# Attention and two gated feed-forward layers on one core: chunk 2 of layer 0 in block products, x summed by VectorE, a later rounding, and GpSimd in part of the decode

## The chip, the cores and the metric

One of the eight cores of a Trainium2 chip runs the whole program. TensorE (PE) multiplies, VectorE (DVE), ScalarE (ACT) and GpSimd (POOL) work on tiles, SyncE (SP) issues loads; each engine takes its instructions in order, and semaphores tie them together. The metric is the device time of one execution in microseconds, the median of the runs.

## The reference

Sliding-window attention with a few global keys and a distance bias, then two feed-forward layers on its output. The weights come as float64. In short:

```python
a = softmax(q @ k.T / sqrt(D) + bias, masked to local and global keys)   # B=2, H=8, S=768, D=64
x = (a @ v) as 1536 tokens x 512
h = x @ w_in1;  x = (h * sigmoid(h)) @ w_out1           # w_in 512 x 2048, w_out 2048 x 512
h = x @ w_in2;  out = (h * clip(h + 3, 0, 6) / 6) @ w_out2
```

## The kernel before, in words

**Precision.** Each operand of a feed-forward matmul is a pair, a rounded high half and the low half that is left (xh and xl, wih and wil, woh and wol, gh and gl). A product takes three matmuls: high by high, high by low, low by high. A matmul here is 128 x 128 by 512 columns.

**Stages.** Attention runs first, in 16 units, with the first feed-forward chunk already between its steps. A layer has 8 chunks of 256 hidden columns, and the tokens are three blocks of 512. For a chunk, an H piece (L489, 12 matmuls, in a PSUM tile psH) makes 128 hidden rows of a block, the gate follows on ScalarE and VectorE, and a Y piece (L662, 6 matmuls, psY) brings it back to 128 output rows or tokens. Y is copied to a tile st by ScalarE (L687) and added to the tile y by an accumulating DMA from GpSimd's queue (L691).

**Block products.** In chunks for which `fast` says so, blocks 0 and 1 are not made by four H pieces but by seven products of six matmuls (L570, tiles psP, a scheme of the Strassen kind), in the order 1, 6, 5, 7, 2, 4, 3. They use sums of blocks of x (T2, T3, T4 and an overwritten part of xh and xl, made in `block_sums`: L621 on VectorE, roundings L594 or L596 on ScalarE, low halves L599 on VectorE) and sums of weights (`sums`: L169 to L181 and L193). Product 1 goes into chain a; ScalarE copies it to chain b (L575) before product 6 adds to it, and copies b to a tile u after products 6 and 7 (L579, L581). Products 2 and 4 end in gates of block 0; products 5, 7 and 3 and u give block 1. The Y pieces of blocks 1 and 2 of the chunk before (eight after a fast chunk, four otherwise) stand between the products where the list `cuts` puts them. Block 2 is made by two H pieces behind them.

**Decode.** The float64 weights of a chunk come in four pieces (two of w_in, two of w_out), loaded by SP (L87, L90). For each, ScalarE takes the magnitude of the upper word (L103), VectorE clamps, shifts, sets the sign and takes the power (L992, L998, L1004, L1009), scales the lower word (L129), adds (L134), ScalarE rounds to the high half (L145) and the low half is subtracted (L148). The engine of L134 and L148 is GpSimd for the two chunks beside the attention and VectorE otherwise. `load_weights` issues a later piece's load once L129 has read its buffer.

**Order.** The program is a list `stream` of pieces; a slot n of the loop records one piece for TensorE and what has been put down for n: the queue (`at`, `split`), `late`, `rests`, and the decode steps (`slots`), which count back from the first piece of their chunk. In the late part the order on all four engines is that of the recording. `ready` picks the PSUM banks of H and Y pieces. At the end of layer 0, `split` with the table `wait` rounds the new x from y: ScalarE's L596 for xh, VectorE's L599 for xl, two for each block.

Of the kernel before, what the change touches and what calls it, by code (L numbers as in the profile page):

```python
# [10 lines left out]
F32 = mybir.dt.float32  # L11
# [17 lines left out]
def attention_ffn_kernel(ctx, tc, q, k, v, n_global, n_local, w_in1, w_out1, w_in2, w_out2, out):  # L29
# [63 lines left out]
    def decode(n):  # L93
# [2 lines left out]
        t = {}  # L96

        beside_attention = i < 2
        engine = nc.gpsimd if beside_attention else nc.vector

        def upper():
            t["a"] = wpool.tile([P, DW], F32, name=f"da{n}", tag="da", bufs=2)
# [51 lines left out]

    def fast(l, c):

        return c > (2, 1)[l]

    terms = {}

# [446 lines left out]
    def whole_block(b):  # L607

        T["x", b] = late_pool.tile([P, KT, FB], F32, name=f"xf{b}", tag=("g1", "ws")[b])
        h, o = (x.bitcast(F32)[:, :, b * FB:(b + 1) * FB] for x in (xh, xl))  # L610
        nc.sync.dma_start(T["x", b], h)
        nc.gpsimd.dma_start(T["x", b], o, accum_op=ALU.add)

    def block_sums(l, n, n1):

# [32 lines left out]
    def y_piece(l, c, tk, m):  # L648
# [16 lines left out]
        for i, ts, size in parts(n0, n1):  # L665
# [28 lines left out]
                    at(n + 9 + j, lambda j=j: nc.scalar.mul(y[:, j, :], y[:, j, :], 1.0 / 6.0))  # L694
            if c == NCH - 1:

                wait = ((6, 6), (5, 5), (4, 3))[i][m // 2]
                split(n + wait, *(x[:, m - 1:m + 1, n0:n1] for x in (xh, xl)), y, 0.5)


# [4 lines left out]
    for l, c in chunks:  # L705
        first_piece[l, c] = len(stream)
        if fast(l, c):
            p = [(product, l, c, i) for i in (1, 6, 5, 7, 2, 4, 3)]
            y, before = before, []
            cuts = [0, 2, 3, 4, 5, 6, 7, 8] if len(y) == 8 else [0, 1, 2, 3, 3, 4, 4, 4]  # L710
            for i in range(7):
                stream += [p[i]] + y[cuts[i]:cuts[i + 1]]
            h, y = H(l, c, 2), Y(l, c, 0)
            stream += [h[0]] + y[:2] + [h[1]] + y[2:]
            before = Y(l, c, 1) + Y(l, c, 2)
            continue
# [64 lines left out]
    with tc.manual_schedule(engines={E.PE, E.Activation, E.Pool, E.DVE}):  # L781

        first_half.close()
        late_pool = second_half.enter_context(tc.tile_pool(name="late", bufs=1, side="right", reuse_waits="tile"))
        for b in range(2):
            whole_block(b)
        for n in range(end, when(len(stream) - 1) + 2):
            if n == when(first_piece[0, 3]):
                ready[0] = 2
            for l, c, early in ((0, 2, 0), (1, 1, 6)):  # L790
                if n == when(first_piece[l, c]) - early:
                    block_sums(l, n, n + early + 12)
            loop(n)
            if n == PRE + 60:
                general = nc.values_load(flag[0:1, 0:1], min_val=0, max_val=2)
# [246 lines left out]
```

## Time and profile before

| | |
|---|---|
| median of 3 runs | 624.74 us (624.72 to 626.45) |
| profiled execution | 625.65 us, its span 623.5 us |
| TensorE clock granted | 0.998 of full speed |
| attention, with chunk 0 beside it | up to about 130 us |
| chunk 2 of layer 0, first H piece | 165.5 us |
| chunk 3 of layer 0, first product | 198.1 us |
| layer 1, first H piece | 358.1 us |
| chunk 2 of layer 1, first product | 423.0 us |
| last matmul of the last Y piece | 617.8 us |

The times in the trace are microseconds from the span's start. A number in brackets behind a row is idle time of that engine just before the instruction, and the engine, tile and line that ended it. Matmuls overlap, so a row's duration (0.39) is longer than the distance to the next. Line numbers are those of the listing above.

### The profile page before, as it was taken

What the parts mean: (1) busy time and instruction counts of PE and PEld (TensorE: products, weight loads), DVE (VectorE), ACT (ScalarE), POOL (GpSimd) and SP (SyncE); (2) the same over time, 40 slices, a digit from 0 to 9 for tenths busy, and PEclk for the clock granted to TensorE, in tenths of its full rate; (3) what the DMA queues carried; (4) which work ended last, traced back from release to release, by engine and by line L of the source; (5) the groups of instructions that cost most, each with busy time, mean ns of one, the idle gap of its engine ahead of it and who ended that gap; (6) DMA issues with size and microseconds to landing.
All of it is one profiled execution on the core that took longest, in us unless ns stands there. A gap on an engine that the chain in (4) does not pass through costs nothing.

```text
span 623.5 us, 9408 instructions
## 1 busy us (share of the span) xinstructions
PE 605.3 (97%) x3128; PEld 494.9 (79%) x3128; DVE 470.6 (75%) x1044; ACT 414.7 (67%) x863; POOL 158.0 (25%) x233
## 2 busy tenths in 40 slices
PE   8899999999999999999999989999999999999996
PEld 3577788898887888888888868887788888888885
DVE  6888888725697776767665789987979696969453
ACT  4888888655576666666656766756667676767660
POOL 3877566820111111111111210011111111111100
PEclk9999999999999999999999999999999999999999
DMA  7767655484776768777876772378577868786544
GB/s 176 178 157 167 155 143 124 138 181 114 159 150 153 182 149 183 155 180 155 183 156 147 173 171 70 126 198 189 124 177 157 184 153 181 155 185 138 102 110 165
DMA packets 81622, 97.29 MB, mean 156 GB/s; under 512 B 55456, under 2 KB 55456, under 8 KB 81312
## 3 DMA queue, kind: packets, MB, share of 16 engines
q0 software_dynamic: 12576, 45.09, 38.6%
q1 hardware_dynamic: 68992, 51.53, 28.3%
q8 instruction: 27, 0.44, 0.3%
q14 instruction: 27, 0.22, 0.1%
HBM read 46.27 MB, written 3.15 MB: 79 GB/s over the span
## 4 chain that ended last, share of the span: by engine, by line
PE 36%; issue 25%; POOL 5%; DVE 2%; DMA 2%; ACT 1%; POOLq 0%; ACTq 0%; SPq 0%; DVEq 0%
PE psY L662 20%; PE psH L489 9%; POOL y L691 5%; PE psP_b L570 3%; PE psP_c L570 2%; PE psP_a L570 2%; DMA y<-st 1%; DMA raw<-in_moe_w_in_dram 1%; ACT st L687 0%; DVE g L520 0%; DVE da L1004 0%; DVE wol L148 0%; DVE u L587 0%; DVE dc L134 0%; ACT da L103 0%
## 5 line engine op out<-in xcount | busy, mean ns | idle before, releaser
L691 POOL DMA_DIRECT2D y<-st x78 | 66.9, 857 | 364.6 <-ACT st L687 359.4
L687 ACT COPY st<-psY 128x512 f32<-128x512 f32 x156 | 91.3, 585 | 52.1 <-PE psY L662 48.0
L489 PE MATMUL psH<-xh,wih 128*128 128x512 f32 (+1 forms) x216 | 83.0, 384 | 2.2 <-DVE g L520 1.8
L489 PE MATMUL psH<-xl,wih 128*128 128x512 f32 (+1 forms) x216 | 82.6, 383 | 0.1
L489 PE MATMUL psH<-xh,wil 128*128 128x512 f32 (+1 forms) x216 | 82.5, 382 | 0.0
L662 PE MATMUL psY<-gh,woh 128*128 128x512 f32 (+1 forms) x160 | 61.4, 384 | 0.6 <-DVE mn L379 0.6
L662 PE MATMUL psY<-gh,wol 128*128 128x512 f32 (+1 forms) x160 | 60.6, 379 | 0.0
L662 PE MATMUL psY<-gl,woh 128*128 128x512 f32 (+1 forms) x160 | 60.5, 378 | 0.0
L662 PE MATMUL psY<-woh,gh 128*128 128x512 f32 x144 | 56.1, 390 | 0.4 <-ACT gh L526 0.4
L662 PE MATMUL psY<-woh,gl 128*128 128x512 f32 x144 | 56.1, 390 | 0.2 <-DVE gl L533 0.2
L662 PE MATMUL psY<-wol,gh 128*128 128x512 f32 x144 | 56.0, 389 | 0.0
L383 ACT ACTIVATE z<-z,mn 128x256 f32<-128x256 f32 (+1 forms) x96 | 46.4, 488 | 10.9 <-DVE mn L379 10.6
L393 POOL TENSOR_SCALAR z<-z,sm 128x256 f32<-128x256 f32 (+1 forms) x96 | 43.5, 471 | 32.3 <-DVE sm L389 25.0
L489 PEld LDWEIGHTS psH<-xh,wih 128*128 128x128 f32 x216 | 40.6, 188 | 10.4 <-DVE g L520 2.2
L103 ACT ACTIVATE da<-raw 128x512 f32<-128x512 f32 x64 | 43.0, 672 | 6.8 <-DMA raw<-in_moe_w_in_dram 5.6
L489 PEld LDWEIGHTS psH<-xl,wih 128*128 128x128 f32 x216 | 40.5, 188 | 7.9 <-DVE xl L425 0.5
L1004 DVE SCALAR_TENSOR_TENSOR da<-raw,da 128x512 int32<-128x512 int32 x64 | 46.0, 718 | 1.0
L489 PEld LDWEIGHTS psH<-xh,wil 128*128 128x128 f32 x216 | 40.6, 188 | 7.5 <-POOL wil L148 0.3
L992 DVE TENSOR_SCALAR da<-da 128x512 f32<-128x512 f32 x64 | 29.1, 454 | 16.2 <-ACT da L103 16.1
L587 DVE TENSOR_TENSOR u<-psP_c,u 128x512 f32<-128x512 f32 x22 | 15.1, 687 | 34.5 <-ACT u L581 34.5
L511 ACT ACTIVATE a<-psH 128x512 f32<-128x512 f32 (+1 forms) x24 | 14.2, 590 | 40.5 <-PE psH L489 38.7
L530 DVE SCALAR_TENSOR_TENSOR gl<-a,gh 128x512 fp32r<-128x512 f32 (+1 forms) x34 | 23.2, 681 | 22.3 <-ACT gh L524 22.0
(187 smaller groups left out, 1499.8 us busy)
## 6 DMA issues: line engine op xcount, KB each, us to landing
y<-st POOLq DMA_DIRECT2D x78, 512.0 KB, 4.9
raw<-in_moe_w_in_dram SPq DMA_DIRECT2D x32, 512.0 KB, 4.3
raw<-in_moe_w_out_dram SPq DMA_DIRECT2D x32, 512.0 KB, 3.6
rk<-in_k_dram SPq DMA_DIRECT2D x32, 96.0 KB, 3.2
rq<-in_q_dram SPq DMA_DIRECT2D x32, 96.0 KB, 2.7
rv<-in_v_dram SPq DMA_DIRECT2D x32, 96.0 KB, 2.6
out_dram<-y SPq DMA_DIRECT2D x12, 256.0 KB, 2.3
xf<-xh SPq DMA_DIRECT2D x2, 1024.0 KB, 4.8
```

Of the source, the lines that this page charges most:

```text
L103: nc.scalar.activation(out=t["a"], in_=raws[n][:, :, 1].bitcast(F32), func=AF.Abs)
L383: nc.scalar.activation(out=z[:, t, h, :w], in_=z[:, t, h, :w], func=AF.Exp, bias=mn[:, t, h:h + 1], scale=-1.0, accum_out=sm[:, t, h:h + 1])
L393: nc.gpsimd.tensor_scalar(out=z[:, t, h, :w], in0=z[:, t, h, :w], scalar1=smt[u][:, t, h:h + 1], scalar2=1.0, op0=ALU.mult, op1=ALU.mult)
L489: nc.tensor.matmul(ps, a[:, kt, js], x[:, kt, n0:n1], start=n == 0, stop=n == 3 * KT - 1)
L530: nc.vector.scalar_tensor_tensor(out=gl[:, j, :], in0=t["a"], scalar=2.0, in1=gh[:, j, :].bitcast(F32), op0=ALU.mult, op1=ALU.subtract)
L570: nc.tensor.matmul(ps, a[:, 2 * k + q, f * P:(f + 1) * P], x, start=p in (1, 5) and n == 0, stop=n == 5, skip_group_check=True)
L587: nc.vector.tensor_tensor(out=u, in0=st["c"], in1=u, op=ALU.add)
L662: nc.tensor.matmul(ps[:, :rhs.shape[1]], lhs, rhs, start=n == 0, stop=n == 3 * FC - 1)
L687: nc.scalar.copy(st[:, m % 2, :], part)
L691: late.setdefault(n, []).append(lambda: nc.gpsimd.dma_start(y, st, accum_op=ALU.add))
L992: nc.vector.tensor_scalar(out=a, in0=a, scalar1=as_float(897 << 20), scalar2=as_float((1151 << 20) - 1), op0=ALU.max, op1=ALU.min)
L1004: nc.vector.scalar_tensor_tensor(out=ai, in0=w1, scalar=-0x40000000, in1=ai, op0=ALU.bitwise_and, op1=ALU.bitwise_or)
```

## The change

Four things change.

- `fast` takes in chunk 2 of layer 0. Its blocks 0 and 1 become seven products; the block sums of layer 0 are recorded from the end of the attention on, their last rounding four slots ahead of the chunk, and the banks are switched at chunk 2, not 3. The decode of the chunk gets the lead that fast chunks have, and the weight sums.
- `whole_block` puts xh + xl together with four VectorE instructions of 128 x 1024, where a load on SP's queue and an accumulating DMA on GpSimd's did it for each block.
- `cuts` for four Y pieces puts two of them between product 1 and product 6 and none between product 6 and product 5. The rounding of block 2 of the new x is recorded at slots 5 and 5 behind its Y pieces, not 4 and 3.
- In layer 1, chunks 1 to 3 have L134 and L148 on GpSimd (24 instructions).

```diff
-        engine = nc.gpsimd if beside_attention else nc.vector
+        engine = nc.gpsimd if beside_attention or NCH < i < NCH + 4 else nc.vector
...
-        return c > (2, 1)[l]
+        return c > 1
...
-        nc.sync.dma_start(T["x", b], h)
-        nc.gpsimd.dma_start(T["x", b], o, accum_op=ALU.add)
+        for k in range(0, KT, 2):
+            h, o = (x.bitcast(F32)[:, k:k + 2, b * FB:(b + 1) * FB] for x in (xh, xl))
+            nc.vector.tensor_tensor(out=T["x", b][:, k:k + 2], in0=h, in1=o, op=ALU.add)
...
-                wait = ((6, 6), (5, 5), (4, 3))[i][m // 2]
+                wait = ((6, 6), (5, 5), (5, 5))[i][m // 2]
...
-            cuts = [0, 2, 3, 4, 5, 6, 7, 8] if len(y) == 8 else [0, 1, 2, 3, 3, 4, 4, 4]
+            cuts = [0, 2, 3, 4, 5, 6, 7, 8] if len(y) == 8 else [0, 2, 2, 3, 3, 4, 4, 4]
...
-            if n == when(first_piece[0, 3]):
+            if n == when(first_piece[0, 2]):
                 ready[0] = 2
-            for l, c, early in ((0, 2, 0), (1, 1, 6)):
-                if n == when(first_piece[l, c]) - early:
-                    block_sums(l, n, n + early + 12)
+            if n == end:
+                block_sums(0, n + 1, when(first_piece[0, 2]) - 4)
+            if n == when(first_piece[1, 1]) - 6:
+                block_sums(1, n, n + 18)
```

Three places in the order of instructions show it. The first is ScalarE at the start of chunk 2 of layer 1, from the copy of product 1 (tile psP_2_a) into chain b; st_1_2 are the old Y pieces of block 2. Before:

```order
L575 COPY psP_2_b<-psP_2_a 128x512
L687 COPY st_1_2_0_4789<-psY_1_1024_0_4782 128x512
L579 COPY u_2_4777<-psP_2_b 128x512
L687 COPY st_1_2_0_4789<-psY_1_1024_1_4803 128x512
L103 ACTIVATE da_4818<-raw_4715 128x512
```

and after:

```order
L575 COPY psP_2_b<-psP_2_a 128x512
L687 COPY st_1_2_0_4796<-psY_1_1024_0_4789 128x512
L687 COPY st_1_2_0_4796<-psY_1_1024_1_4800 128x512
L579 COPY u_2_4784<-psP_2_b 128x512
L103 ACTIVATE da_4825<-raw_4722 128x512
```

The copy out of product 6 (L579) has moved behind the second Y piece's copy, as product 6 has on TensorE.

The second is VectorE early in layer 1's chunk 0, where y_2 is the new x of block 2 and g_0_0_1 the gate that frees the second H piece's bank. Before:

```order
L1009 TENSOR_SCALAR de_4254<-da_4186 128x512
L599 SCALAR_TENSOR_TENSOR xl<-y_2_2124,xh 128x2x512
L520 SCALAR_TENSOR_TENSOR g_0_0_1_4259<-a_0_0_1_4251,psH_0_0_1_4238 128x512
L129 SCALAR_TENSOR_TENSOR dc_4279<-raw_4064,de_4254 128x512
L992 TENSOR_SCALAR da_4256<-da_4256 128x512
L533 TENSOR_TENSOR gl_0_0_4204<-g_0_0_1_4259,gh_0_0_4203 128x512
```

and after (the decode helpers stand one line further down there, so L1010 is L1009 and L993 is L992):

```order
L1010 TENSOR_SCALAR de_4260<-da_4193 128x512
L520 SCALAR_TENSOR_TENSOR g_0_0_1_4265<-a_0_0_1_4257,psH_0_0_1_4244 128x512
L129 SCALAR_TENSOR_TENSOR dc_4285<-raw_4071,de_4260 128x512
L993 TENSOR_SCALAR da_4262<-da_4262 128x512
L599 SCALAR_TENSOR_TENSOR xl<-y_2_2131,xh 128x2x512
L533 TENSOR_TENSOR gl_0_0_4211<-g_0_0_1_4265,gh_0_0_4210 128x512
```

The low half of the new x (L599) has moved behind the gate; its second half stands eight rows further down.

The third is GpSimd from the end of layer 0 on. L638 are two transfers that start layer 1's sums y, and they wait until the block sums have read that tile's old content (the last reader is the low half t4l). Before:

```order
L691 DMA y_2_2124<-st_7_2_0_4167 128x1024
L691 DMA y_2_2124<-st_7_2_2_4219 128x1024
L638 DMA y_0_4536<-yf_4317 128x2048
L638 DMA y_1_4538<-yf_4396 128x2048
L691 DMA y_0_4536<-st_1_0_0_4598 128x1024
```

and after:

```order
L691 DMA y_2_2131<-st_7_2_2_4226 128x1024
L134 TENSOR_TENSOR dc_4285<-dc_4285,da_4193 128x512
L148 TENSOR_TENSOR wil_4337<-dc_4285,wih_4336 128x512
L134 TENSOR_TENSOR dc_4353<-dc_4353,da_4262 128x512
L148 TENSOR_TENSOR wil_4337<-dc_4353,wih_4336 128x512
L134 TENSOR_TENSOR dc_4422<-dc_4422,da_4341 128x512
L148 TENSOR_TENSOR wol_4469<-dc_4422,woh_4468 128x512
L134 TENSOR_TENSOR dc_4492<-dc_4492,da_4409 128x512
L638 DMA y_0_4543<-yf_4322 128x2048
L638 DMA y_1_4545<-yf_4403 128x2048
L148 TENSOR_TENSOR wol_4469<-dc_4492,woh_4468 128x512
```

Decode steps now stand between the transfers, and the last low half of chunk 1's w_out stands behind L638.

## Rows read from the trace of the kernel before

**Rows 1.** The page, part 1: busy us, share, instructions of each engine.
```profile
PE 605.3 (97%) x3128; PEld 494.9 (79%) x3128; DVE 470.6 (75%) x1044; ACT 414.7 (67%) x863; POOL 158.0 (25%) x233
```

**Rows 2.** TensorE over time: start us, us, line, tile, instructions [idle before <-releaser].
```profile
187.25 0.39 PE L489 MATMUL psH<-xh,wih 128*128 128x512 f32 x1
...
189.97 0.39 PE L662 MATMUL psY<-gh,woh 128*128 128x512 f32 x1
...
200.62 0.39 PE L662 MATMUL psY<-gh,wol 128*128 128x512 f32 x1
201.51 0.50 PE L570 MATMUL psP_b<-t2h,ws 128*128 128x512 f32 x1 [0.50 <-ACT psP_b L575]
...
369.00 0.39 PE L489 MATMUL psH<-xh,wil 128*128 128x512 f32 x1
371.15 0.50 PE L489 MATMUL psH<-xh,wih 128*128 128x512 f32 x1 [1.76 <-DVE g L520]
...
393.04 0.39 PE L662 MATMUL psY<-woh,gh 128*128 128x512 f32 x1
...
426.38 0.50 PE L570 MATMUL psP_b<-t2h,ws 128*128 128x512 f32 x1 [0.53 <-ACT psP_b L575]
...
442.68 0.50 PE L662 MATMUL psY<-woh,gh 128*128 128x512 f32 x1 [0.37 <-ACT gh L526]
...
443.56 0.51 PE L662 MATMUL psY<-woh,gl 128*128 128x512 f32 x1 [0.15 <-DVE gl L533]
```

**Rows 3.** Chain that ended last, one of its longest pieces: start us, us, what.
```profile
359.26 8.90 DMA y<-st
```

**Rows 4.** ScalarE over time, ahead of the waits at 371 and 442.
```profile
368.18 1.06 ACT L596 ACTIVATE xh<-y 128x1024 fp32r<-128x1024 f32 x1 [2.26 <-DMA y<-st]
...
439.17 0.67 ACT L515 ACTIVATE a<-psP_b,three 128x512 f32<-128x512 f32 x1
```

**Rows 5.** VectorE over time: a block sum, then the same two places.
```profile
166.69 1.22 DVE L621 TENSOR_TENSOR t1f<-xf,xf 128x1024 f32<-128x1024 f32 x1
...
369.27 1.22 DVE L599 SCALAR_TENSOR_TENSOR xl<-y,xh 128x1024 fp32r<-128x1024 f32 x1 [2.00 <-ACT xh L596]
...
391.77 0.68 DVE L533 TENSOR_TENSOR gl<-g,gh 128x512 fp32r<-128x512 f32 x1
...
433.33 0.43 DVE L992 TENSOR_SCALAR da<-da 128x512 f32<-128x512 f32 x1 [2.92 <-ACT da L103]
...
440.36 0.68 DVE L134 TENSOR_TENSOR dc<-dc,da 128x512 f32<-128x512 f32 x1
440.96 0.42 DVE L992 TENSOR_SCALAR da<-da 128x512 f32<-128x512 f32 x1
441.30 0.68 DVE L520 SCALAR_TENSOR_TENSOR g<-a,psP_b 128x512 f32<-128x512 f32 x1
```

**Rows 6.** Stretches, all engines: us busy (instructions), granted clock, DMA share, GB/s.
```profile
core 0: us, PE busy (x) PEld busy (x) DVE busy (x) ACT busy (x) POOL busy (x), PEclk, DMA share, GB/s
126.00:165.00 39.00, 39.00 (x188) 34.07 (x187) 17.58 (x32) 22.02 (x46) 6.58 (x6) 1.00 0.71 148
371.00:404.00 33.00, 32.85 (x145) 27.21 (x146) 32.33 (x53) 22.04 (x36) 1.09 (x2) 1.00 0.27 89
```

**Rows 7.** VectorE from 371 to 404 by line: xcount | busy us, mean ns.
```profile
L134 DVE TENSOR_TENSOR dc<-dc,da 128x512 f32<-128x512 f32 x5 | 3.4, 682 | 0.0
...
L148 DVE TENSOR_TENSOR wil<-dc,wih 128x512 fp32r<-128x512 f32 x2 | 1.4, 688 | 0.0
```

**Rows 8.** GpSimd up to 130 us by line, same columns.
```profile
L134 POOL TENSOR_TENSOR dc<-dc,da 128x512 f32<-128x512 f32 x8 | 10.7, 1334 | 0.3
```

**Rows 9.** VectorE beside GpSimd during the attention, and the same line alone.
```profile
114.92 1.72 POOL L134 TENSOR_TENSOR dc<-dc,da 128x512 f32<-128x512 f32 x1
...
115.88 1.04 DVE L1009 TENSOR_SCALAR de<-da 128x512 int32<-128x512 int32 x1
...
139.69 0.42 DVE L1009 TENSOR_SCALAR de<-da 128x512 int32<-128x512 int32 x1
```

More of the change, by code (lines that the diff above doesn't have):

```diff
@@ L609, in whole_block @@
         T["x", b] = late_pool.tile([P, KT, FB], F32, name=f"xf{b}", tag=("g1", "ws")[b])
-        h, o = (x.bitcast(F32)[:, :, b * FB:(b + 1) * FB] for x in (xh, xl))
-        nc.sync.dma_start(T["x", b], h)
-        nc.gpsimd.dma_start(T["x", b], o, accum_op=ALU.add)
+        for k in range(0, KT, 2):
+            h, o = (x.bitcast(F32)[:, k:k + 2, b * FB:(b + 1) * FB] for x in (xh, xl))
+            nc.vector.tensor_tensor(out=T["x", b][:, k:k + 2], in0=h, in1=o, op=ALU.add)
     def block_sums(l, n, n1):
```

## The prediction

> **What bounds the kernel now.** I read the page's first part first: TensorE is busy 605.3 us of the span, VectorE 470.6, ScalarE 414.7 [rows 1]. So a microsecond counts only where TensorE issues fewer matmuls or stops waiting. Then TensorE over time, for its pace: the twelve matmuls of an H piece start at 187.25 and the next piece at 189.97, so one takes 2.72 / 12 = 0.227 us [rows 2]. Then the same view for its stops after the attention. Four places carry nearly all of them [rows 2]: 201.51 (the b chain of chunk 3 waits for ScalarE's copy L575), 371.15 (an H piece of layer 1's chunk 0 waits for VectorE's gate L520), 426.38 (as 201.51, in layer 1's chunk 2) and 442.68 to 443.56 (that chunk's first Y piece waits for gh and gl). Against the pace the second costs 371.15 - 369.00 - 0.23 = 1.92. At 201.51 the same reckoning gives 0.89 - 0.23 = 0.66 where the bracket shows 0.50, since the end of a matmul is modelled; adding that 0.16 to the brackets of the others gives 0.69 at 426.38, 0.53 at 442.68 and 0.31 at 443.56. The matmul right behind a stop is 0.1 slower too. So: 0.77, 2.0, 0.80 and 1.06 us.
>
> Behind 371.15 stands a transfer: an accumulation issued at 359.26 takes 8.90 us [rows 3]; ScalarE's rounding L596 waits 2.26 us for it [rows 4], VectorE's L599 2.00 us for that, and the gate that frees the PSUM bank stands behind L599 in VectorE's queue [rows 5]. Behind 442.68 stands VectorE alone: its gate on psP_b starts at 441.30 [rows 5], though ScalarE has its input ready at 439.17 + 0.67 = 439.84 [rows 4].
>
> **The change part by part.** *Six matmuls fewer.* Chunk 2 of layer 0 makes blocks 0 and 1 by 7 products of 6 matmuls in place of 4 H pieces of 12: 42 for 48, on the path throughout: 6 x 0.227 = **-1.36 us**.
>
> *What chunk 2 needs earlier.* Its T tables must be there by 165 us. VectorE adds x in four instructions of 1024 columns, and the eight instructions of the block sums (the first at 166.69, 1.22 us [rows 5]) move ahead by a chunk; with the weight sums of the chunk (four quarter sums and two low halves, 4 x 0.42 + 2 x 0.69 = 3.1 us) that is 12 x 1.22 + 3.1 = 17.7 us more between 126 and 165, where VectorE is busy 17.58 of 39 us [rows 6]. It fits, with 3.7 to spare; nothing is charged. ScalarE is busy 22.02 there and gains three roundings of T and three product copies. The two loads on SP's queue and the two accumulations on GpSimd's go; nothing waited for them.
>
> *One Y piece more before the b chain.* With four old Y pieces the cut list now sets two between product 1 and product 6, not one: 1.36 us more for L575, against waits of 0.77 and 0.80. In layer 0 the short list falls to chunk 2, whose ScalarE queue is like chunk 3's now, and chunk 3 gets the list of eight, which had two Y pieces already: **-0.77**. In layer 1's chunk 2 the 0.80 goes too, but 16 us later the same chunk waits for the gate on psP_b, which hangs on VectorE and not on TensorE. What TensorE gains at 426 it waits at 442 unless VectorE comes earlier. So 0.80 and 1.06 belong to the last part.
>
> *The later rounding.* L596 and L599 of y_2 now stand behind the bank's gate. The H piece in question ends near 369.00 - 2.72 + 0.23 = 366.5; L515 (0.67) and the gate (0.68) can follow at once, the transfer landing at 368.16 or not, so the bank is free by 368.1, ahead of 369.23: **-2.0**. Next in line is the second L599. The third H piece now ends at 371.95; the gates, roundings and low halves of two tiles take turns behind it until near 375.4, then L596 (1.06) and L599 (1.22) end near 377.7. The first reader is the eighth matmul of that block's H piece, after four Y pieces: 371.95 + 4 x 1.36 + 1.59 = 379.0. That is 1.3 us of cover; what runs past it comes back.
>
> *GpSimd in the decode.* Of each of 12 weight pieces the add L134 and the low half L148 go to GpSimd: 24 instructions. VectorE is rid of 0.60 each (start to start, 440.36 to 440.96 [rows 5]). GpSimd takes about 1.3 for one [rows 8]. What does one cost VectorE meanwhile? During the attention a VectorE L1009 took 1.04 beside GpSimd's L134, but 0.42 alone [rows 9]: it ended 0.28 after GpSimd's instruction, so it was held until that was over. Eight such instructions, this the last of them, were held there 3.7 us in all, beside 30 two-operand GpSimd instructions: 0.13 us for each. But there VectorE mostly read PSUM. From 371 to 404 it is busy 32.33 of 33 us [rows 6], nearly all between SBUF tiles. So the cost b of a moved instruction lies between 0.13 and about 1.28. If the two engines took turns, b would be near 1.1 (1.28 less the share of PSUM gates and idle time); if GpSimd gets in only when VectorE reads PSUM for 0.68 us, b is about 0.60 and nothing is won or lost. I take 0.85, midway. From 371 to 404 nine instructions leave VectorE (five L134, as shown, and four L148) [rows 7]: 9 x (0.85 - 0.60) = 2.25 us later. Against that stand 0.67 us of idle time and the lead of the tightest consumer: the gl low half at 391.77 ends at 392.45 [rows 5], and the Y piece that starts at 393.04 [rows 2] reads it in its sixth matmul, 1.13 later: 1.72. Together 2.39, so TensorE just doesn't notice. Queued behind the two transfers L638, which wait for t4l, is the last low half of layer 1's chunk 1's w_out, which that chunk's first Y pieces read; it comes no earlier than t4l allows. At 442 the way from VectorE's restart at 433.33 [rows 5] to the gate holds four moved instructions; one GpSimd does while VectorE stands idle, three contend: 3 x 0.25 = **+0.75**, and neither 0.80 nor 1.06 is won.
>
> Sum: -1.36 - 0.77 - 2.0 + 0.75 = **-3.4 us**. The profiled execution took 625.65 us (span 623.5, 2.15 around it); the median is 624.74, 0.9 lower, at the same work. 624.74 - 3.4 = **621.3**.
>
> **The rivals.** *The lock (slower).* GpSimd and VectorE take full turns, b = 1.28. Then 371 to 404 costs 9 x 0.68 - 2.39 = 3.73 us of TensorE's time, seen as waits of Y pieces for gl near 390 and for the wol low half behind L638 near 402, and the way to 442 costs 3 x 0.68 = 2.04: -4.13 + 5.77 = +1.6, so 626.4. It decides where 9 (b - 0.6) - 2.39 + 3 (b - 0.6) reaches 4.13: from b = 1.14 on the kernel is slower. For it: VectorE has 0.67 us idle in 33, and the held L1009. Against it: no row shows who goes first when VectorE has its next instruction ready. The Trainium skill ("SBUF — State Buffer", Who interferes with whom) states such a lock: a VectorE instruction with two SBUF inputs, or in a two-port mode, and a GpSimd instruction that reads SBUF exclude each other for the whole instruction. By that rule the time is this rival's; the trace agrees in the held L1009 (1.04 against 0.42), and the page leaves open, too, who wins when VectorE is never idle.
>
> *GpSimd fits in (more is won).* b stays at the attention's 0.13. VectorE comes 4 x 0.47 = 1.9 us earlier to the gate at 441.30, which is 1.46 late now: both layer 1 waits go, another 1.86 on top of -4.13: 618.7. For it: the rows of the attention. Against: VectorE's load there was of another kind.
>
> *Chunk 2 comes late.* The 3.7 us spare before 165 are an average; VectorE's queue is in order and waits for ScalarE's T roundings and gh. If the low half of the weight sums is 2 us behind its product, the gain is 4.13 - 0.75 - 1.7: 623.0. For it: 35 of 39 us busy. Against: the last of these instructions is due only four products in, and VectorE catches up in its idle time.
>
> **How the numbers follow.** About 0.3%, 1.9 us, is what a measurement of this kernel can tell from no change. Chances: the forecast 50% (its own range, b from 0.6 to 1.0, is 620.6 to 623.0), the lock 22% (624 to 626.5), GpSimd fits in 18%, chunk 2 late 10%. Faster than 622.9: 48 of the forecast, the 18, and 2 of chunk 2: 68%. Slower than 626.6: the upper end of the lock: 11%. Between: 21%. The range from 618.5 to 625.6 leaves out a few per cent below and most of the upper half of the lock.
>
> **What would show it.** Right: no stop before psP_b in chunks 2 and 3 of layer 0 or in chunk 2 of layer 1; H pieces of layer 1's chunk 0 without the 1.8 us; 42 matmuls on psP tiles in chunk 2. For b: the mean of VectorE's L1004, L129 and the clamp, shift and power lines between 370 and 450, now 0.68 and 0.42, and whether Y pieces of layer 1's chunks 0 to 2 wait for gl, wol or gh. Wrong: a stop between 126 and 180 for a T table or ws, or GpSimd instructions much longer than 1.3 us, with weights that come late.

## The result and the profile after

The changed kernel takes 633.35 us (median of 6 runs, 631.77 to 636.03) where the kernel before took 625.51 beside it: 1.0131 of its time, with an interval of 1.0111 to 1.0150. It is 1.3% slower. 621.3 was forecast, with 625.6 as the upper end.

The profiled execution took 635.12 us, its span is 633.0 (before: 623.5). First the page's part 1, which answers [rows 1]:

```profile
PE 609.9 (96%) x3122; PEld 496.6 (78%) x3122; DVE 485.6 (77%) x1032; ACT 417.1 (66%) x868; POOL 194.3 (31%) x255
```

TensorE issues 6 matmuls fewer, as planned, and is still busy 4.6 us longer, mostly since some of them run at a low clock (below). VectorE has lost 24 instructions to GpSimd and gained 12 in layer 0, and is busy 15.0 us longer. GpSimd has gained 36.3.

TensorE over time, where it stops (columns as in [rows 2]):

```profile
180.83 0.50 PE L570 MATMUL psP_b<-t4h,wih 128*128 128x512 f32 x1 [2.32 <-ACT u L581]
181.87 0.63 PE L570 MATMUL psP_b<-t4l,wih 128*128 128x512 f32 x1
...
395.78 0.50 PE L662 MATMUL psY<-woh,gl 128*128 128x512 f32 x1 [0.80 <-DVE gl L533]
...
407.35 0.50 PE L662 MATMUL psY<-wol,gh 128*128 128x512 f32 x1 [0.62 <-POOL wol L148]
...
439.74 0.50 PE L570 MATMUL psP_b<-t4h,wih 128*128 128x512 f32 x1 [1.38 <-ACT u L581]
...
447.79 0.55 PE L662 MATMUL psY<-woh,gl 128*128 128x512 f32 x1 [1.84 <-DVE gl L533]
...
449.37 0.80 PE L662 MATMUL psY<-woh,gh 128*128 128x512 f32 x1 [1.03 <-ACT gh L526]
```

Of the four stops in [rows 2], those at 201.51 and 371.15 have gone, as forecast, and that at 426.38 nearly so. In their place stand three kinds of new ones. Two lie ahead of product 4, at 180.83 and 439.74, and wait for ScalarE's copy L581. Two are Y pieces of layer 1 that wait for gl and for a low half made by GpSimd, at 395.78 and 407.35. The pair at 447.79 and 449.37 has grown out of the 1.06 at 442.68 and 443.56. Added up against the pace of 0.2275 as in the prediction, the stops behind the attention make 5.2 us before and 15.0 after, matmuls at low clock included. Less 1.36 for the six matmuls, that is some 8.5 of the 9.5 us between the spans. Another 0.6 lies behind the last Y matmul: from its start to the end of the span it is 6.3 us, in before 5.7.

Two stops are followed by a low clock. TensorE by stretches (from and to, length, us busy and instructions, granted clock, DMA share, GB/s), two of them behind the stops at 180.83 and 449.37:

```profile
175.00:178.30 3.30, 3.30 (x16) 1.00 0.92 256
182.00:185.00 3.00, 3.00 (x9) 0.50 0.00 0
...
450.40:454.50 4.10, 4.10 (x11) 0.50 0.00 0
```

The granted clock is 1.00 ahead of the stop and 0.50 behind it, which is 1.2 of 2.4 GHz: some 1.6 us lost on top of the first stop and 3 on the last two.

### The profile page after: what moved, and what is told of

The parts are those of the page before. It is cut to its first block, busy times and chain, and to the rows that moved or that the text cites. A ratio compares the mean times of both kernels' runs of the same rounds, so it can differ in the third digit from the quotient of the medians.

```text
span 633.0 us, 9415 instructions
## 1 busy us (share of the span) xinstructions
PE 609.9 (96%) x3122; PEld 496.6 (78%) x3122; DVE 485.6 (77%) x1032; ACT 417.1 (66%) x868; POOL 194.3 (31%) x255
## 3 DMA queue, kind: packets, MB, share of 16 engines
q0 software_dynamic: 11520, 43.00, 36.3%
## 4 chain that ended last, share of the span: by engine, by line
PE 81%; DVE 8%; DMA 4%; ACT 3%; issue 2%; POOL 0%; DVEq 0%; SPq 0%; ACTq 0%; POOLq 0%
PE psY L662 37%; PE psH L489 19%; PE psP_b L570 7%; PE psP_c L570 5%; PE psP_a L570 4%; DMA raw<-in_moe_w_in_dram 3%; PE psO L421 2%; PE psT L403 2%; PE psS_S L369 2%; DVE da L1005 1%; PE psA L329 1%; PE psW L430 1%; DVE z L379 1%; DVE de L1010 1%; PE psS_o L369 1%
## 5 line engine op out<-in xcount | busy, mean ns | idle before, releaser
L691 POOL DMA_DIRECT2D y<-st x78 | 67.9, 871 | 333.9 <-ACT st L687 322.7
L489 PE MATMUL psH<-xh,wih 128*128 128x512 f32 (+1 forms) x200 | 77.0, 385 | 0.5 <-ACT y L676 0.5
L489 PE MATMUL psH<-xl,wih 128*128 128x512 f32 (+1 forms) x200 | 76.7, 383 | 0.2 <-DVE xl L425 0.2
L489 PE MATMUL psH<-xh,wil 128*128 128x512 f32 (+1 forms) x200 | 76.5, 383 | 0.0
L662 PE MATMUL psY<-gh,woh 128*128 128x512 f32 (+1 forms) x152 | 58.3, 383 | 0.7 <-DVE mn L379 0.7
L662 PE MATMUL psY<-gl,woh 128*128 128x512 f32 (+1 forms) x152 | 57.4, 378 | 0.0
L662 PE MATMUL psY<-gh,wol 128*128 128x512 f32 (+1 forms) x152 | 57.4, 378 | 0.0
L103 ACT ACTIVATE da<-raw 128x512 f32<-128x512 f32 x64 | 42.9, 671 | 16.2 <-DMA raw<-in_moe_w_in_dram 14.1
L993 DVE TENSOR_SCALAR da<-da 128x512 f32<-128x512 f32 x64 | 30.8, 481 | 22.4 <-ACT da L103 22.4
L1005 DVE SCALAR_TENSOR_TENSOR da<-raw,da 128x512 int32<-128x512 int32 x64 | 46.0, 719 | 1.9 <-DVE da L993 0.9
L129 DVE SCALAR_TENSOR_TENSOR dc<-raw,de 128x512 f32<-128x512 uint32 x56 | 43.5, 778 | 0.8
L489 PEld LDWEIGHTS psH<-xl,wih 128*128 128x128 f32 x200 | 37.8, 189 | 7.6 <-DVE xl L425 0.5
L489 PEld LDWEIGHTS psH<-xh,wil 128*128 128x128 f32 x200 | 37.7, 188 | 6.9 <-POOL wil L148 0.3
L526 ACT CAST gh<-g 128x512 fp32r<-128x512 f32 (+1 forms) x42 | 25.5, 608 | 21.6 <-DVE g L520 21.1
```

Of the source, the lines that this page charges most:

```text
L103: nc.scalar.activation(out=t["a"], in_=raws[n][:, :, 1].bitcast(F32), func=AF.Abs)
L129: nc.vector.scalar_tensor_tensor(out=t["c"], in0=raws[n][:, :, 0].bitcast(U32), scalar=2.0 ** -52, in1=t["e"].bitcast(F32), op0=ALU.mult, ...
L489: nc.tensor.matmul(ps, a[:, kt, js], x[:, kt, n0:n1], start=n == 0, stop=n == 3 * KT - 1)
L526: nc.scalar.copy(gh[:, j, :], t["g"])
L662: nc.tensor.matmul(ps[:, :rhs.shape[1]], lhs, rhs, start=n == 0, stop=n == 3 * FC - 1)
L691: late.setdefault(n, []).append(lambda: nc.gpsimd.dma_start(y, st, accum_op=ALU.add))
```

## Where product 4 waits in the changed kernel

ScalarE and VectorE at the start of chunk 2 of layer 0 (product 1 starts at 165.71), with GpSimd's and SP's issues; it answers [rows 4, 5] for a place that the prediction didn't look at:

```profile
179.16 0.66 ACT L103 ACTIVATE da<-raw 128x512 f32<-128x512 f32 x1 [6.85 <-DMA raw<-in_moe_w_in_dram]
179.72 0.57 ACT L687 COPY st<-psY 128x512 f32<-128x512 f32 x1
180.19 0.59 ACT L581 COPY u<-psP_b 128x512 f32<-128x512 f32 x1
...
169.53 0.43 DVE L993 TENSOR_SCALAR da<-da 128x512 f32<-128x512 f32 x1 [0.71 <-ACT da L103]
170.84 0.69 DVE L1005 SCALAR_TENSOR_TENSOR da<-raw,da 128x512 int32<-128x512 int32 x1 [0.88 <-DVE da L993]
...
171.40 0.90 POOL L691 DMA_DIRECT2D y<-st  x1 [3.02 <-ACT st L687]
...
173.49 0.38 SPq L87 DMA_DIRECT2D raw<-in_moe_w_in_dram  x1
```

ScalarE's L581, which frees chain b for product 4, is short and its input is long there. It stands in order behind L103, which takes the magnitude of the next chunk's raw words, and these land late. Two things go into that, both visible above. The accumulation L691 of the two old Y pieces is issued at 171.40, ahead of the raw load at 173.49, since both pieces now stand directly behind product 1. And the load itself is issued late: it stands behind L129, L129 behind L1005, and there VectorE is idle for 0.88 us. The order of instructions has the register load of the flag just there (the slot of the loop is fixed by number, and chunk 2's product 1 now falls on it). In layer 1's chunk 2 the first of the two repeats, at 439.74.

## The experiments

All ratios are to the kernel before, run beside each on the same chip, in brackets the 95% interval.

| run | what it is | us | ratio |
|---|---|---|---|
| e1 | after, GpSimd out of layer 1 | 628.96 | 1.0051 [1.0034, 1.0069] |
| e2 | before, GpSimd alone | 631.10 | 1.0084 [1.0067, 1.0101] |
| e3 | before, cuts and rounding | 629.40 | 1.0055 [1.0038, 1.0071] |
| e4 | before, chunk 2 alone | 626.32 | 1.0011 [0.9992, 1.0029] |
| e12 | before, rounding alone | 625.13 | 0.9982 [0.9973, 0.9992] |
| e5 | e3, magnitude behind L581 | 625.28 | 0.9992 [0.9980, 1.0005] |
| e6 | e3, second copy behind L579 | 623.82 | 0.9965 [0.9954, 0.9976] |
| e7 | before, 24 more GpSimd instructions | 635.77 | 1.0163 [1.0129, 1.0197] |
| e8 | e1, magnitudes later, flag earlier | 621.57 | 0.9934 [0.9912, 0.9956] |
| e9 | e1, second copy behind L579 | 628.93 | 1.0050 [1.0034, 1.0066] |
| e13 | e1, flag earlier | 629.53 | 1.0051 [1.0034, 1.0068] |
| e10 | e1, both | 623.73 | 0.9964 [0.9952, 0.9977] |
| e14 | after, both (GpSimd kept) | 630.73 | 1.0061 [1.0046, 1.0077] |
| e11 | e10, leads 17 and 13 | 623.36 | 0.9954 [0.9941, 0.9967] |
| e15 | e10, gate a slot earlier | 623.25 | 0.9963 [0.9944, 0.9982] |

### The change taken apart

Without GpSimd in layer 1:

```diff
-        engine = nc.gpsimd if beside_attention or NCH < i < NCH + 4 else nc.vector
+        engine = nc.gpsimd if beside_attention else nc.vector
```

> The changed kernel with the add and the low half of layer 1's chunks 1 to 3 back on VectorE. Theory (GpSimd and VectorE hold each other up): the stops at 395.78 (1.07), 407.35 (1.21) and from 447.79 to 455 (2.00 + 1.35 and about 3 us of half clock behind them) go, 8.6 us of 633.4: about 624.5; the stop ahead of product 4 in layer 0's chunk 2 stays (2.6, and 1.6 at half clock), that in layer 1's chunk 2 (1.6) may go or stay, 623 to 625. Rival (the transfers and the new cut list do the harm, GpSimd only stands by): within 1.5 us of the changed kernel, 632 to 633, with the stops after 440 still there.

628.96, which neither theory had: of the 1.31% GpSimd accounts for 0.80, and 0.51 stay. The Y pieces no longer stop at 395 and 407, but the stop ahead of product 4 in layer 1 is still there (1.74), and 2.5 us near 444 with half clock behind it too, so that part wasn't GpSimd's work. The reverse edit, in the kernel before:

> The kernel before with only the 24 instructions moved to GpSimd. Theory: the stops of the changed kernel between 371 and 455 appear here as they stand, 1.07 + 1.21 + 6.3, less the waits of 0.80 and 1.06 that were there anyhow: 6 to 8 us slower than before, 631 to 633.5. Rival (transfers and cuts): within 1 us of the kernel before, 624.5 to 626.5. Of the forecast's own arithmetic (0.85 us of VectorE for each moved instruction): 626.2.

631.10, at the low end of the first theory: 0.84% for 24 moved instructions. The profiled execution is the fastest of the four (629.04). The other two parts alone: e3 is the kernel before with the two table entries below, e4 the kernel before with `fast`, `whole_block` and the block sums of the change.

```diff
-                wait = ((6, 6), (5, 5), (4, 3))[i][m // 2]
+                wait = ((6, 6), (5, 5), (5, 5))[i][m // 2]
...
-            cuts = [0, 2, 3, 4, 5, 6, 7, 8] if len(y) == 8 else [0, 1, 2, 3, 3, 4, 4, 4]
+            cuts = [0, 2, 3, 4, 5, 6, 7, 8] if len(y) == 8 else [0, 2, 2, 3, 3, 4, 4, 4]
```

> The kernel before with only the new cut list and the later last rounding. The short list falls to chunk 3 of layer 0 here, and to chunk 2 of layer 1. As forecast for these two parts: the waits of 0.77 and 2.0 go, the 0.80 turns up again 16 us later: 622.7 (625.5 less 2.8). Rival (two old Y pieces straight behind product 1 put their accumulation ahead of the raw load, whose landing ScalarE's copy to u waits for): a stop of 1.5 to 2.6 us ahead of product 4 in layer 0's chunk 3 and in layer 1's chunk 2, with half clock behind it: 625 to 627.

> The kernel before with only chunk 2 of layer 0 in block products and x put together by VectorE; old cut list, old rounding, no GpSimd in layer 1. If the stop ahead of product 4 (2.6, and 1.6 at half clock) comes with the chunk itself (raw loads that land late beside three accumulations, and VectorE held up at product 1): 625.5 - 1.4 + 4.2 = about 628; the wait at 201.51 goes if chunk 3's list of eight serves it: 627.5. If it comes from the new cut list: no such stop, 1.36 and the 0.77 of chunk 3 won and 0.77 lost ahead of chunk 2's product 6: about 624.

e3 takes 629.40, the rival and more: the two parts that were forecast to bring 2.8 us cost 0.55%. The stops at 201 and 371 go, and 1.75 (at 212.23) and 1.81 (at 437.23) come ahead of product 4, with 1.09 and 2.5 behind them:

```profile
212.23 0.50 PE L570 MATMUL psP_b<-t4h,wih 128*128 128x512 f32 x1 [1.49 <-ACT u L581]
...
437.23 0.50 PE L570 MATMUL psP_b<-t4h,wih 128*128 128x512 f32 x1 [1.54 <-ACT u L581]
```

e4, between its two cases, is within what can be told from no change. There is no stop ahead of product 4 in it, which clears the chunk itself, but one of 1.71 ahead of product 6: in the chunk's first microseconds L575 stands behind an L103 that waits 1.09 us for its raw words. That and 0.58 at 186 eat the 1.36 and the 0.77. Its rows (SP and GpSimd, then ScalarE, VectorE and TensorE):

```profile
162.46 0.38 SPq L87 DMA_DIRECT2D raw<-in_moe_w_in_dram  x1
161.53 0.85 POOL L691 DMA_DIRECT2D y<-st  x1 [5.15 <-ACT st L687]
...
168.42 0.66 ACT L103 ACTIVATE da<-raw 128x512 f32<-128x512 f32 x1 [1.09 <-DMA raw<-in_moe_w_in_dram]
168.98 0.58 ACT L575 COPY psP_b<-psP_a 128x512 f32<-128x512 f32 x1
...
170.41 0.69 DVE L1005 SCALAR_TENSOR_TENSOR da<-raw,da 128x512 int32<-128x512 int32 x1 [0.88 <-DVE da L993]
...
169.61 0.50 PE L570 MATMUL psP_b<-t2h,ws 128*128 128x512 f32 x1 [1.44 <-ACT psP_b L575]
```

The load is issued 0.93 us behind an accumulation and takes 5.94. The flag's load, at 170.41, is later than this stop and no part of it.

Of e3's parts the rounding alone:

> The kernel before with only the later last rounding. As forecast: the stop at 371.15 goes and nothing takes its place, 2.0 us faster. Rival (the second low half or a later wait takes part of it back): 0.5 to 1.2 us faster.

In the trace the stop at 371 is gone, 2.0 us, and the stops add up to 3.2 where before has 5.2, so nothing took its place. The medians show less, 0.18% (0.5 to 1.7 us). The last Y matmul starts 2.2 us earlier than in before, but from there to the end of the span it is 6.5 us and not 5.7, which takes 0.8 back in this execution; over the 17 traces that way is 5.7 to 6.7 us, and before's is the shortest. So all that e3 loses is the cut list's, by the medians some 4.5 us.

### Why ScalarE's copy is late

Two edits to e3 tell the queue from the transfer. The first leaves the load late and takes L103 out of L581's way (the end of a longer line):

```diff
-((20, 15, 11, 6), (18, 14, 9, 2))[fast(*chunks[i])][j]
+((20, 15, 11, 6), (18, 14, 9, 2), (18, 11, 9, 2))[2 if chunks[i] in ((0, 4), (1, 3)) else fast(*chunks[i])][j]
```

> The kernel with the new cut list and the later rounding alone (629.4), where in the two chunks with the short list ScalarE's magnitude L103 of the next chunk's second w_in piece is put behind the copy L581 instead of ahead of it (lead 11 for 14). Theory (product 4 waits for a copy that is queued in order behind an L103 whose raw words land late): the stops of 1.75 at 212 and 1.81 at 437 go; the words land as late as there, so VectorE still gets them late and part of the later stops (1.09 at 219, 2.5 near 445) may stay: 622.5 to 626. Rival (L581 is late for another reason, chain b or VectorE): 628.5 to 629.5, the stops as they were.

(With lead 11 the weight sums, which are made in place, come before the piece's weights are rounded, so these two chunks multiply by other numbers. Kind, size and number of the instructions stay.) 625.28, 0.63% less than e3. ScalarE over time, in e5:

```profile
208.03 0.59 ACT L581 COPY u<-psP_b 128x512 f32<-128x512 f32 x1 [0.77 <-PE psP_b L570]
...
210.61 0.66 ACT L103 ACTIVATE da<-raw 128x512 f32<-128x512 f32 x1 [1.48 <-DMA raw<-in_moe_w_in_dram]
```

L581 waits for TensorE alone and product 4 doesn't stop in either layer, though the words come as late as in e3 (L103 at 210.56 there). VectorE still gets them late, and the stop ahead of gl, 1.09 at 219 in e3, stays (1.20 at 218). So it is through ScalarE's queue that the late words hold up product 4; the later stop comes from the words themselves, by way of VectorE. The second edit moves the copy, and with it the accumulation, back to where it was:

```diff
+            if (l, c, i, m) in ((0, 2, 2, 1), (1, 1, 2, 1)):
+                def after_product_6():
+                    nc.scalar.copy(st[:, 1, :], part)
+                    nc.gpsimd.dma_start(y, st, accum_op=ALU.add)
+                late.setdefault(n + 1, []).append(after_product_6)
+                continue
```

> The same kernel (new cut list and later rounding, 629.4), where the second old Y piece keeps its place on TensorE but is copied out by ScalarE behind product 6's copy L579, as before the change, so that its accumulation is issued about 2 us later, behind the raw load of L87 and not ahead of it. Theory (two transfers in turn: which was issued first decides when the raw words land): the raw load lands 3.6 us behind its issue as before, not 5.9, the wait of L103 is 2 to 3 us and not 6, and the stops at 212, 219, 437 and 445 go: 622.5 to 624. Rival (the load is late whatever goes ahead of it, or TensorE's new order delays chain b): 628 to 629.5.

623.82, better than the kernel before by 0.35%: both stops ahead of product 4 are gone, and that ahead of gl with them; near 440 it stops for 1.9 us, where before has 1.06. The chain of waits shows the load itself (start, us from issue to landing), at first in e3, in both layers:

```profile
204.33 6.15 DMA raw<-in_moe_w_in_dram
...
429.26 6.22 DMA raw<-in_moe_w_in_dram
```

and in e6, in layer 1:

```profile
426.48 3.66 DMA raw<-in_moe_w_in_dram
```

The same 512 KB, once behind an accumulation of 512 KB and once ahead of it. The runs together:

| place | raw load issued | accumulation issued | load takes |
|---|---|---|---|
| before, layer 1 | 428.94 | 430.32 | 3.62 |
| e6, layer 1 | 426.48 | 427.57 | 3.66 |
| e10, layer 0 | 171.86 | 172.45 | 3.62 |
| e9, layer 0 | 175.70 | 175.34 | 5.14 |
| after, layer 0 | 173.49 | 171.40 | 5.59 |
| e1, layer 0 | 173.21 | 171.10 | 4.40 |
| e13, layer 0 | 172.10 | 170.87 | 6.10 |
| e3, layer 0 | 204.33 | 203.50 | 6.15 |

Half a microsecond on either side decides over 1.5 to 2.5 us. The order isn't all: e1 has the same instructions in layer 0 as the changed kernel and nearly the same distance, and its load takes 1.2 us less, which is why its stop there is 1.44 and not 2.6. Each row is one execution.

### The flag

e9 puts e6's edit into the changed kernel without GpSimd (in layer 0 on the Y pieces of chunk 1, since the short list now falls to chunk 2), e10 also moves the register load, e13 has that alone:

```diff
-            if n == PRE + 60:
+            if n == PRE + 45:
                 general = nc.values_load(flag[0:1, 0:1], min_val=0, max_val=2)
```

> The changed kernel without GpSimd in layer 1 (629.0), with the second old Y piece of the short lists copied out behind product 6's copy L579, as in the run of the copy put later. Theory (a raw load behind an accumulation, and an in-order L103 ahead of L581): of its stops 1.44 at 179, 1.08 at 187, 1.74 at 435 and about 3 us of stop and half clock from 441 to 449 go: 621.5 to 623.5; the 0.34 at 170 stays. Rival (chunk 2 of layer 0 comes late by itself, as it did alone, where nothing was won): 624 to 626.

> The same kernel, with the load of the flag into the registers 15 slots earlier, where the changed kernel has it at product 1 of chunk 2 and VectorE stands idle 0.88 us around it. If that idle time is part of why the raw load of chunk 3 is issued late: 0.3 to 1 us faster than the same kernel without it, by a stop of up to 0.5 at 170 to 187. If not: the same within 0.3.

> The changed kernel without GpSimd in layer 1 (629.0), with the flag's load 15 slots earlier and the copy of the second Y piece as changed. Theory (what counts is which transfer is issued first): in layer 0's chunk 2 the raw load is issued some 0.9 us earlier, but the accumulation still goes ahead of it, so L103 ends 0.9 us earlier and of the stop of 1.44 ahead of product 4 about 0.6 stays; the stops of layer 1 (1.74 at 435 and what follows) stay as they are: 627 to 628.5. Rival (the flag alone is the cause in layer 0): no stop ahead of product 4 there.

e9 missed: 628.93. The stop in layer 1 is gone, but ahead of product 4 in layer 0 there are still 2.1 us. e13 missed as well: the stop there is 2.1, not 0.6. Only both edits together remove it, and the table above says why. The flag costs VectorE 1 us (e9 here, then e10):

```profile
171.75 0.43 DVE L999 TENSOR_SCALAR da<-da 128x512 f32<-128x512 f32 x1 [0.71 <-ACT da L103]
173.06 0.69 DVE L1011 SCALAR_TENSOR_TENSOR da<-raw,da 128x512 int32<-128x512 int32 x1 [0.88 <-DVE da L999]
```

```profile
168.89 0.43 DVE L999 TENSOR_SCALAR da<-da 128x512 f32<-128x512 f32 x1 [0.71 <-ACT da L103]
169.23 0.69 DVE L1011 SCALAR_TENSOR_TENSOR da<-raw,da 128x512 int32<-128x512 int32 x1
```

In e9 that microsecond puts the raw load 0.36 behind the accumulation, in e10 it is 0.59 ahead. What the flag's move is worth is less than the 5.2 us between the medians: e9's profiled execution reaches product 6 of chunk 2 2.9 us later than e10's (172.26 against 169.39), which the flag can't cause: most of it is lost in the first 45 us, where e9's granted clock is 0.96 and e10's 1.00. From there to the end of the span it is 453.2 against 450.7, so 2.5 us. e9's other executions had granted clocks of 0.993 to 0.996; whether they lost at the start or behind the stop, their times don't show.

### What GpSimd costs

e7 leaves VectorE all its work and lets GpSimd do as many instructions beside it that nobody waits for:

```diff
+        def beside(x):
+            if NCH < i < NCH + 4:
+                s = late_pool.tile([P, DW], mybir.dt.bfloat16, name=f"scratch{n}_{now[0]}", tag="scratch")
+                nc.gpsimd.tensor_tensor(out=s, in0=x, in1=x, op=ALU.add)
...
+            beside(t["a"])
...
+            beside(t["h"].bitcast(F32))
```

> The kernel before (626.3 on this chip) with 24 additional GpSimd instructions of 128x512 beside layer 1's chunks 1 to 3, one behind each L134 and L148 of VectorE, whose result nobody reads; VectorE keeps all its work. They cost what they hold VectorE up and nothing else. Theory by the busy times so far (VectorE's sum with the moved instructions is 0.92 us for each above what is left to it): 9 x 0.92 - 2.4 = 5.9 from 371 to 404 and 3 x 0.92 = 2.8 to 442, 8 to 9 us slower: 633 to 636. Full turns (1.28): 9.1 + 3.8, 638 to 639. Rival (VectorE isn't held; what costs in the changed kernel is that GpSimd's results come late): 625.5 to 627.5.

635.77, as the theory has it: 10 us for 24 results that no one reads. So it is the holding that costs, not that GpSimd's results come late. Nor do the accumulations leave later for the instructions ahead of them in GpSimd's queue: between 358 and 530 all but one are issued 0.29 to 0.31 us behind ScalarE's copy, as in before. VectorE is busy 488.0 us where before has 470.6: 0.73 for each. Where GpSimd really does the work, VectorE's rows in e2 show it (VectorE, then GpSimd, from 436 on):

```profile
437.20 1.41 DVE L1009 TENSOR_SCALAR de<-da 128x512 int32<-128x512 int32 x1
...
439.73 1.89 DVE L129 SCALAR_TENSOR_TENSOR dc<-raw,de 128x512 f32<-128x512 uint32 x1
...
442.14 1.76 DVE L533 TENSOR_TENSOR gl<-g,gh 128x512 fp32r<-128x512 f32 x1
...
444.16 0.68 DVE L520 SCALAR_TENSOR_TENSOR g<-a,psP_b 128x512 f32<-128x512 f32 x1
```

```profile
436.50 1.82 POOL L148 TENSOR_TENSOR wol<-dc,woh 128x512 fp32r<-128x512 f32 x1 [1.77 <-ACT woh L145]
...
439.47 1.59 POOL L148 TENSOR_TENSOR wil<-dc,wih 128x512 fp32r<-128x512 f32 x1
...
441.70 1.66 POOL L134 TENSOR_TENSOR dc<-dc,da 128x512 f32<-128x512 f32 x1 [0.64 <-DVE dc L129]
```

Each of these GpSimd instructions holds one VectorE instruction until it is over: 437.20 + 1.41 = 438.61, 0.29 behind GpSimd's 438.32. The three take 0.99, 1.21 and 1.08 us more than in before (0.42, 0.68, 0.68). A gate that reads PSUM passes, and the instruction behind it is held (e2, VectorE and then GpSimd):

```profile
396.68 0.68 DVE L520 SCALAR_TENSOR_TENSOR g<-a,psH 128x512 f32<-128x512 f32 x1
397.28 0.93 DVE L992 TENSOR_SCALAR da<-da 128x512 f32<-128x512 f32 x1
...
395.71 2.21 POOL L134 TENSOR_TENSOR dc<-dc,da 128x512 f32<-128x512 f32 x1 [1.09 <-DVE dc L129]
```

Counted over all of e2's rows between 358 and 530, 22 VectorE instructions for 24 of GpSimd are held, 20.0 us in all: 0.83 us for each of the 24, and 1.06 for the seven between 372 and 406, where VectorE is never idle. GpSimd's own mean is 1.50 us there, where it had 1.334 in [rows 8].

Last, the changed kernel with the copy and the flag mended and GpSimd kept:

> The changed kernel with the flag's load earlier and the copy behind L579, GpSimd kept in layer 1's chunks 1 to 3; without GpSimd the same kernel takes 623.7. Theory (GpSimd and VectorE hold each other up, whatever the transfers do): stops of Y pieces near 392 and 404 (0.3 to 1.2 each) and 2 to 4 us near 444, with or without half clock behind them: 627 to 630. Rival (GpSimd costs only where raw words land late): 623.5 to 625.

630.73, just above the 627 to 630 of the theory, where the same kernel without GpSimd (e10) takes 623.73: 0.97% by the ratios, 6 to 7 us. Its trace has the Y pieces' stops at 391 to 393 (1.5) and 404 (1.2), and 3.3 near 443 with a stretch of half clock behind them.

### Versions that take up what was learned

e8 has the earlier flag and, for chunk 3 of layer 0 and of layer 1, other leads:

```diff
-((20, 15, 11, 6), (18, 14, 9, 2))[fast(*chunks[i])][j]
+((20, 15, 11, 6), (18, 14, 9, 2), (16, 11, 9, 2))[2 if chunks[i] in ((0, 3), (1, 3)) else fast(*chunks[i])][j]
```

> The changed kernel without GpSimd in layer 1 (629.0), with two more edits: in the chunks with the short list the next chunk's two w_in magnitudes L103 stand behind L575 and L581 (leads 16 and 11 for 18 and 14), and the load of the flag into the registers stands 15 slots earlier, not at product 1 of chunk 2. Theory (in-order queues behind late raw words): of its stops the 0.34 at 170, 1.44 at 179, 1.08 at 187, 1.74 at 435 and most of 4.5 from 441 to 449 go: 620 to 623, better than the kernel before. Rival (the words land late in any case and VectorE pays): 626 to 629.

621.57, within the expectation, but its lead of 11 changes the weights as in e5, so it is no version to use. The two that follow start from e10 and leave the weights as they are: e11 with (17, 13, 9, 2) in that place, e15 with the gate and the low half behind product 4 recorded earlier in the two chunks 2 (`soon`):

```diff
-            rests.setdefault(now[0] + wait + 1, []).append(gate)
+            (late if soon else rests).setdefault(now[0] + wait + (not soon), []).append(gate)
...
-        rests.setdefault(now[0] + wait + 2, []).append(lo)
+        (late if soon else rests).setdefault(now[0] + wait + 2 - soon, []).append(lo)
```

> The kernel with the earlier flag, with the decode of the next chunk's w_in one slot later in the two chunks with the short list (leads 17 and 13 for 18 and 14): the first L103 stands behind L575, and one add of VectorE less stands ahead of the gate on psP_b. Theory (what is left are in-order queues): the stop of 0.34 at 170 goes, and of about 2.0 near 440 some 0.6: 0.5 to 1.2 us faster than with leads 18 and 14. Rival (the steps only move the wait, since the raw words land when they land): the same within 0.4.

> The kernel with the earlier flag and the later copy (623.7), in which behind product 4 of the two chunks 2 VectorE's gate and low half are put ahead of one slot's decode steps. Theory (the stop near 438 hangs on VectorE's queue): the gate comes 0.9 us earlier, the stops of 1.25 and 0.42 there shrink to about 0.7, that of 0.76 at 184 goes: 1.0 to 1.8 us faster, 622 to 622.7. Rival (the decode steps put back make the next weights late): the same or slower.

623.36 and 623.25 against e10's 623.73: the same. In e11 the stop at 170 has gone; near 439 its two stops make 2.0 us, where e10 has 1.7. In e15 the gate comes earlier and the first stop shrinks from 1.25 to 0.6, but the one behind it, for gl, grows from 0.42 to 1.02: VectorE has the same work there in any order. So the best versions are e6, e10, e11 and e15, all 0.35 to 0.46% faster than the kernel before, and not told apart from each other.

## Why the prediction was wrong, step by step

**The bound.** That TensorE's stops are the place to look was right: some 8.5 of 9.5 us are read from them.

**Six matmuls fewer.** Right: 42 on the psP tiles, and e10 has the six fewer. They weren't won alone (e4), because of the next step.

**"Nothing is charged" for chunk 2's earlier start.** This step failed. The part that was reckoned held: VectorE is busy 30.4 us from 126 to 165, where the step had 17.6 + 17.7, and no product waited for a T table or a weight sum. What was left out is the decode of the next chunk, which now runs through a chunk with products: ScalarE's L103 stands ahead of L575 and L581 and waits for its raw words. In e4 the first of these loads takes 5.94 us behind an accumulation, which costs 1.7 us at product 6; no run changed that alone. With the new cuts the second load is late too, behind an accumulation and asked for by a VectorE queue that now holds the flag's load: 2.6 and 1.6 of half clock at product 4 in the changed kernel. The rival "chunk 2 comes late" had the place but not the cause: it looked at the weight sums.

**One Y piece more before the b chain.** The waits of 0.77 and 0.80 went, as said, and still this was the second step that failed. It moved a Y piece and priced its matmuls, but the piece also issues a copy and an accumulation, which came 2 us earlier (203.50 for 205.46 in chunk 3) and passed the raw load. The sum missed 1.75 + 1.09 in layer 0 and, of 1.81 + 2.5 in layer 1 (e3), all but the 1.86 that it had expected to stay. [rows 2] held what was needed only on TensorE; the issues of SP and GpSimd beside it would have shown that the load stood 1.4 us ahead of the accumulation, less than the 2 us by which it was moved.

**The later rounding.** Right in mechanism and, in the trace, in size: 2.0 us, with the second L599 no stop (e12). The medians show 1.1. e6, which has this part and the new cut list with the accumulation put back, wins 0.35%, 2.2 of the 2.8 us that were forecast for the two.

**GpSimd.** This is the third step that failed, and the largest miss: 0.75 us was charged, and 5.3 (e2) to 7 (e14 against e10) was measured. The price was nearly right and the sum wasn't. 0.85 us for each moved instruction was taken; 0.83 was measured on average, but 1.06 in the stretch where VectorE is the bound, which is the stretch that the sum was made for. With 1.06 it gives 9 x 0.46 - 2.39 = 1.8 us from 371 to 404 (1.3 with the eight instructions that GpSimd really runs there), and e2's stops there add up to 1.5. On the way to 442 three held instructions cost 3.28 us, not 2.55, and the way began 1.6 us later than in before, so that the gate on psP_b came at 444.16, 2.9 us later than its 441.30. For that 0.75 was charged. The lower end of the price was misread too: during the attention 13 VectorE instructions are held beside the 30 two-operand ones of GpSimd, 7.2 us in all, 0.24 each, so the prediction's eight with 3.7 us weren't all of them. The forecast didn't go by that end, but the rival by which GpSimd fits in did. So the lock was the better rival: its places (near 390, near 402, 442) are the ones that stop, and its 5.8 us stand against 5.3 in e2 and 6 to 7 between e14 and e10. Its price of a full turn was a little high, and that its sum fits so well is in part luck: by the stops of e2's profiled execution its two places make 1.5 us and, over the 1.06 of before, 1.9, where it had 3.73 and 2.04. The span of that execution is 3.4 us longer than before's, at a granted clock of 0.999; the other three took 1.9 to 3.1 us more, at 0.992 to 0.996. The Trainium skill ("SBUF — State Buffer", Who interferes with whom) states that lock, and the trace agrees with it in 22 held instructions, by 0.9 us on average. 22% was too little for a rival that a held row in [rows 9] spoke for and only idle time spoke against.

**What no case had.** Half clock behind the stops: 1.6 and 3 us in the profiled execution of the changed kernel. All cases counted a stop at its own length.

Put together from the medians: mending the two transfers takes the changed kernel from 1.0131 to 1.0061 (e14), 4.4 us; taking GpSimd out takes it on to 0.9964 (e10), 6 to 7 us. What is then left is a gain of 2.3 us in the medians, and of 3.4 between the profiled executions' spans (623.5 and 620.1), where the forecast had 4.1 for the same parts. The 0.7 to the spans is about there: e10 stops for 1.7 us near 439, 0.6 more than the 1.06 of before, for 0.8 at 184 and 0.3 at 169, and the 0.80 at 426, which wasn't counted as won, is. The medians show 1.1 less than the spans because the two profiled executions are no average ones: e10's is its fastest (622.28, 1.45 below the median of 623.73), and before's is 0.4 below the median of 626.03. What makes executions of one kernel differ stays open.

## What to carry to other kernels

When a step moves on one engine, list what it issues on the others and look for what each of these now passes: a transfer that went ahead of another cost that other up to 2.5 us here, and an in-order engine that waits for it holds up everything queued behind. An engine that is busy 98% of a stretch isn't relieved by a neighbour that holds it up for longer (1.06 us here) than the instruction taken off it would have cost (0.60); compare the neighbour's duration with the saved one before counting instructions. Work that is placed by a fixed slot number should be looked up again whenever the program around it gets shorter.

## What the runs showed of the hardware

- A load of 512 KB took 3.4 to 3.7 us when it was issued 0.6 to 1.4 us ahead of an accumulation of 512 KB, and 5.1 to 6.4 when it was issued 0.4 to 1.2 us behind it. At other distances it varies: 0.1 to 0.3 behind it took 4.3 in e8 (171.20) and in before (166.84) and 5.76 in e3 (167.06), and 2.1 behind 5.59 in the changed kernel and 4.40 in e1.
- In e2, 22 of 24 GpSimd instructions on 128x512 tiles each hold one VectorE instruction between SBUF tiles, a one-input one (L1009) as well as a two-input one, by 0.9 us on average. GpSimd's instruction gets longer itself (1.50 us for 1.33). A gate of VectorE that reads PSUM ran beside it in its usual 0.68.
- A register load that stands in VectorE's queue cost it 0.88 us of idle time.
- Behind stops of 2.6 us, and of 3.4 in two pieces, the granted clock was 0.50 for 3 to 5 us. A stop of 2.1 ahead of product 4 in layer 0 was followed by half clock in e13 and by none in e9, and 2.5 us of stops near 445 by half clock in e1 and by none in e3. What decides between them the runs don't show.
